# Attention products grouped by tile shape, with scaling tables in PSUM and constants in the opening

## The chip, the cores and the metric

The kernel runs on one core of one Trainium2 chip. The metric is device time in microseconds (us) of one execution, less is better; it is given as the median of several runs.

The engines have these names in the profile: PE is TensorE's matrix products and PEld its weight loads, DVE is VectorE, ACT is ScalarE, POOL is GpSimd, and SP is the engine that issues most of the DMAs here. Each engine works through its own queue in the order in which the program was written.

## The reference

Three layers follow one another: a linear attention with a decaying state, a mixture of 8 experts with one expert per token, and a dense layer. Only the first is touched by the change.

```python
# r, k, v: (4, 8, 768, 48); w, u: (8, 48)
for t in range(S):
    kt, vt, rt = (k[:, :, t], v[:, :, t], r[:, :, t])
    cur = np.einsum('bhd,bhe->bhde', u[None] * kt, vt)
    y[:, :, t] = np.einsum('bhd,bhde->bhe', rt, state + cur)
    state = w[None, :, :, None] * state + np.einsum('bhd,bhe->bhde', kt, vt)
...
# experts: x is y as (3072, 384)
expert_idx = np.argmax(x @ w_gate, axis=1)
out[mask] = gate_w[mask, None] * (np.maximum(xe @ w1[e], 0.0) @ w2[e])
...
# dense: h = x @ w_in;  out = (h - tanh(h)) @ w_out
```

## The kernel before

The attention is computed in chunks of 128 tokens. There are C = 6 chunks and B = 4 batches, and `seq` lists the 24 tiles (chunk, batch) with the batch running fastest. One tile holds all H = 8 heads of 128 tokens, as HP = 4 pairs j of heads with q = 0 or 1 inside a pair. The two heads of a pair lie at partitions 0 to 47 and 64 to 111.

Inside a chunk the products over time become matrix products. For tile n the kernel does this:

- `load` (from SP) brings r, k and v by token into `n_b` (576 KB) and r and k by dimension into `t_b` (two times 192 KB); five buffers each.
- `scale` (VectorE) multiplies r and k by powers of the decay, from the table `PRK` in SBUF, in one instruction over 1024 columns.
- `scores` (TensorE) forms k by r for each head: 64 rows by 128 columns of the array, the two heads of a pair in two PSUM banks `A0` and `A1`. In float32 each product of the program is two matmul instructions in the trace, so 8 products are "x16".
- `side_rk`, `side_rku` and `side_kh` (GpSimd) form r*k, r*k*u and the decayed k, `kh`. `diag_sum` (VectorE) sums r*k*u, and `diag` (ScalarE) puts the sums on the diagonals of `am` with eight instructions. `mask` (VectorE) copies the scores of later tokens over `am`.
- `state` (TensorE) forms kh by v into the PSUM tile `Pp`, which has a bank of its own. VectorE adds it to `sw`, the decayed old state (GpSimd), and keeps the sum in `Sc`. `state_copy` (ScalarE, two instructions) puts it on the blocks of a padded `Sb`.
- `outp` (TensorE) adds two products into `Yp`: inter, from the state of the earlier chunks, `Sb` by `t_b`, as one 128x128 product for each pair; and intra, v by `am`, 128 rows by 48 columns for each head. The two alternate, two pairs at a time. ScalarE copies `Yp` out in two instructions at its end.

For each chunk of four tiles there follow `logits`, `logits2` and `gate` (the expert of each token), `rank_mm` and `rank_sel` (the token's place in its expert) and `idx_mm`. `xout` transposes a tile's output on TensorE into a PSUM tile of the pool `X`, from which ScalarE copies it, scaled by the gate, to `xs`, and SP stores it. The pool `X` has two slots and also serves the logits. Through all this `w_split` makes two parts of expert weights for later, a cast on ScalarE and a subtraction on VectorE.

The order is written out by hand (`manual_schedule`). Loop step n (0 to 24) issues, in this order: the load of n + 3; `diag_sum` and `scale` of n + 1; `logits`; `outp(n - 1)` and its state copy; one `xout`; `diag(n + 1)`; `scores`, `mask` and `state` of n; GpSimd's products of n + 2; then `logits2`, `gate`, `rank_mm`, `rank_sel` and `idx_mm` of chunks that have come so far; then a `w_split`. `at_step(n, first, fn)` calls `fn` for a chunk `first` steps after its last tile. `keep_warm` issues products that nothing reads. `consts` and `gate_cols` are 24 small GpSimd instructions, issued in step 1.

After the loop the last chunk's logits, gate and ranks follow, while a first group of tokens already passes through an expert (`head1`, `head2`); then come the other experts and the dense layer, both long runs of products on TensorE.

Of the kernel before, what the change touches and what calls it, by code (L numbers as in the profile page):

```python
# [30 lines left out]
def rwkv_moe_moe_kernel(ctx: ExitStack, tc: tile.TileContext, rk_t, rkv, pk, u, wp1, wp2, out):  # L31
# [170 lines left out]
    Sc = [ap_.tile([P, HP, D], F32, name=f"Sc{b}") for b in range(B)]  # L202
    Sb = [ap_.tile([P, HP, P], F32, name=f"Sb{b}") for b in range(B)]
# [3 lines left out]
    PRK = ap_.tile([P, 2, HP, P], F32, name="PRK")  # L207
# [5 lines left out]
    yh = [psy.tile([P, BANK], F32, tag=f"y{d}", name=f"yh{d}")[:, 0:HEAD] for d in range(KD)]  # L213
    Yp = [t.rearrange("p (j t) -> p j t", t=P) for t in yh[0:2]]
    Pb = yh[2]
    Pp = Pb[:, 0:HP * D].rearrange("p (j d) -> p j d", d=D)
# [52 lines left out]
    def tables():  # L269
# [9 lines left out]
        table(nc.gpsimd, PRK[:, 0], pq[:, :, 0:8], pw[:, :, 0:16])  # L279
# [3 lines left out]
        table(nc.vector, PRK[:, 1], ipq[:, :, 0:8], ipw[:, :, 1:17])  # L283
# [19 lines left out]
    def zero_states():  # L303
        for b in range(B):
            nc.scalar.mul(out=Sb[b], in_=ident.unsqueeze(1).to_broadcast([P, HP, P]), mul=0.0)
# [24 lines left out]
    def side_kh(n):  # L330
        kh = at3.tile([P, H, D], F32, tag="kh", name="kh")
        nc.gpsimd.tensor_tensor(out=kh, in0=n_b[n % NB][:, 1], in1=KT, op=ALU.mult)
        st["kh", n] = kh
# [29 lines left out]
    def state(n):  # L363
        c, b = seq[n]
        if c == C - 1:
            return
        kh = st.pop(("kh", n))
        for j in range(HP):
            for q in range(2):
                nc.tensor.matmul(Pp[64 * q:64 * q + D, j, :], lhsT=kh[:, 2 * j + q, :],  # L370
                                 rhs=n_b[n % NB][:, 2, 2 * j + q, :], start=True, stop=True)
        if c == 0:
            nc.vector.tensor_copy(out=Sc[b], in_=Pp)
        else:
            sw = at2.tile([P, HP, D], F32, tag="sw", name="sw")
            nc.gpsimd.tensor_tensor(out=sw, in0=Sc[b], in1=bc(pq[:, :, 8:9], [P, HP, D]), op=ALU.mult)
            nc.vector.tensor_tensor(out=Sc[b], in0=sw, in1=Pp, op=ALU.add)
        st["S", b] = n

    def state_copy(n):  # L380
        c, b = seq[n]
        if c == C - 1:
            return
        for q in range(2):
            nc.scalar.copy(out=Sb[b][64 * q:64 * q + 64, :, 64 * q:64 * q + D], in_=Sc[b][64 * q:64 * q + 64, :, :])

    def outp(n):
        c, b = seq[n]
        am = st.pop(("am", n))
        for j0 in range(0, HP, 2):  # L390
            for j in (j0, j0 + 1):
                if c > 0:
                    nc.tensor.matmul(Yp[j % 2][:, j // 2, :], lhsT=Sb[b][:, j, :], rhs=t_b[n % NB][:, 0, j, :],
                                     start=True, stop=False)
            for j in (j0, j0 + 1):
                for q in range(2):
                    p0 = 64 * q
                    nc.tensor.matmul(Yp[j % 2][p0:p0 + D, j // 2, :], lhsT=n_b[n % NB][:, 2, 2 * j + q, :],
                                     rhs=am[:, q, j, :], start=(c == 0), stop=True)
        if b == 0:  # L400
            st["y", c] = yp.tile([P, HP, B, P], F32, tag="y", name="y")
        for i in range(2):
            nc.scalar.copy(out=st["y", c].rearrange("p (j i) b t -> p i j b t", i=2)[:, i, :, b, :], in_=Yp[i])

    sm = ps1.tile([P, 512], F32, tag="sm", name="sm")
# [203 lines left out]
    def by_token():  # L609

        with tc.tile_pool(name="slow", bufs=1) as sp:
# [3 lines left out]
            for b in range(B):  # L615
                nc.vector.memset(Sc[b], 0.0)
# [5 lines left out]
            for c in range(C):  # L622
                st["y", c] = yp.tile([P, HP, B, P], F32, tag="y", name="y")
                for b in range(B):
# [5 lines left out]
                    with tc.For_i(0, P, 1) as t:  # L630
# [8 lines left out]
                        nc.vector.tensor_add(out=cur, in0=cur, in1=Sc[b])  # L639
# [7 lines left out]
                        nc.vector.tensor_tensor(out=Sc[b], in0=Sc[b], in1=bc(wcol.unsqueeze(2), [P, HP, D]), op=ALU.mult)  # L647
                        nc.vector.tensor_add(out=Sc[b], in0=Sc[b], in1=kv)
# [12 lines left out]
    with tc.manual_schedule():  # L661
        w_cols()
        identity()
        for i in range(2):
# [8 lines left out]
        zero_states()  # L673
        keep_warm(20)
        later_keys()
        load(2)
# [20 lines left out]
        for t in Yp + [Pp]:  # L697
            nc.vector.memset(t, 0.0)
# [3 lines left out]
        for n in range(NN + 1):  # L702
            if n + 3 < NN:
                load(n + 3)
            if n % 2 == 1 and n // 4 < PRE:
                w_load(n // 4, n // 2 % 2)
            if n + 1 < NN:
                diag_sum(n + 1)
                scale(n + 1)
            at_step(n, 2, logits)  # L710
            if 1 <= n <= NN:
                outp(n - 1)
                if n > 1:
                    state_copy(n - 1)
            for m in XOUT.get(n, (n - LAG,)):
                if m >= 0:
                    xout(m)
            if 0 < n < NN - 1:
                diag(n + 1)
            if n < NN:  # L720
# [5 lines left out]
                else:  # L726
                    if n == 1:
                        state(0)
                    state(n)
            if n == 1:  # L730
                state_copy(0)
            if n + 2 < NN:
# [4 lines left out]
                side_kh(n + 2)  # L737
            at_step(n, 3, logits2)
            at_step(n, 3, gate)
# [663 lines left out]
```

## Time and profile before

| | us |
|---|---|
| median of 3 runs | 817.4 |
| lowest and highest | 816.46, 819.32 |
| the profiled execution, its own time | 815.03 |
| its span, from first to last instruction | 812.9 |
| busy in the span: PE, DVE, ACT, POOL | 780.9, 648.6, 526.0, 450.7 |

The span is 2.1 us shorter than the execution's own time. All starts below are counted from the span's start. In a row of the timeline the first number is the start, the second the length from the first start to the last end of the merged instructions, then come engine, line, operation, the tiles as out<-in, their shapes and the count; an idle time ahead of the group, with what ended it, stands in square brackets. Two groups of one engine can overlap by their pipelines, so the difference of two starts is the surer measure of what a group costs. The granted clock (PEclk) is given as a share of 2.4 GHz; TensorE's two levels here are 1.2 and 2.4 GHz.

### The profile page before, as it was taken

Reading aid. Unit: us, or ns where it says so; the run is one execution under the profiler, and the core shown is the slowest. Engines: PE = TensorE matmul, PEld = TensorE weight load, DVE = VectorE, ACT = ScalarE, POOL = GpSimd, SP = SyncE. Lnnn points to the kernel's source line nnn. Section 1 sums busy time; section 2 is a strip of 40 time slices with the busy share of each in tenths; the row PEclk is TensorE's granted clock in tenths of the full one; section 3 lists DMA queues with packets and bytes.
Section 4 is the critical chain, followed back from the end, with each engine's and each line's share of the span. In section 5 each row is a group of like instructions: output and inputs, shape, how many; then the busy total and the mean of one; then the engine's idle time right before and its main releaser. Section 6 shows DMA issues by size and latency. Waiting matters only on the chain.

```text
span 812.9 us, 14403 instructions
## 1 busy us (share of the span) xinstructions
PE 780.9 (96%) x5052; PEld 699.3 (86%) x5052; DVE 648.6 (80%) x1127; ACT 526.0 (65%) x1135; POOL 450.7 (55%) x438
## 2 busy tenths in 40 slices
PE   7789999899999999999999999999999999999995
PEld 6567776699899999999989999999999999999895
DVE  7798988449888888995498888888888888888991
ACT  8778887426454545545587776776777677677770
POOL 7987885127676776775445544434345354343532
PEclk9999999999999999999999999999999999999998
DMA  8979864236689889995400000001000000000000
GB/s 220 268 205 260 219 200 135 89 92 188 199 223 267 268 207 276 321 240 160 136 1 0 1 10 30 2 0 40 1 1 30 10 1 20 21 1 10 30 1 39
DMA packets 34979, 89.88 MB, mean 111 GB/s; under 512 B 5690, under 2 KB 13022, under 8 KB 34896
## 3 DMA queue, kind: packets, MB, share of 16 engines
q1 hardware_dynamic: 30704, 78.87, 34.2%
q0 software_dynamic: 4192, 9.99, 4.1%
q8 instruction: 42, 0.69, 0.4%
q14 instruction: 41, 0.34, 0.2%
HBM read 73.10 MB, written 15.74 MB: 109 GB/s over the span
## 4 chain that ended last, share of the span: by engine, by line
PE 49%; DVE 2%; issue 1%; POOL 1%; ACT 0%; POOLq 0%; DVEq 0%; ACTq 0%
PE h L1239 24%; PE o L1287 22%; PE y L1013 2%; PE hps L988 1%; DVE t L1260 0%; DVE h L1257 0%; DVE h L1258 0%; DVE h L1256 0%; DVE t L1255 0%; POOL out_dram L1300 0%; POOL g L1276 0%; ACT g L1275 0%; POOLq L1398 0%; ACT z L1243 0%; ACT t L1245 0%
## 5 line engine op out<-in xcount | busy, mean ns | idle before, releaser
L1276 POOL TENSOR_TENSOR g<-t,g 128x512 fp32r<-128x512 f32 x93 | 120.4, 1295 | 176.3 <-ACT g L1275 122.6
L1239 PE MATMUL h<-xb,ring 128*128 128x512 f32 x864 | 215.9, 395 | 0.7 <-DVE t L1260 0.7
L1287 PE MATMUL o<-ring,g 128*128 128x384 f32 x1116 | 209.3, 336 | 0.0
L1287 PEld LDWEIGHTS o<-ring,g 128*128 128x128 f32 x1116 | 196.1, 188 | 8.1
L1239 PEld LDWEIGHTS h<-xb,ring 128*128 128x128 f32 x864 | 161.3, 188 | 31.9 <-DVE t L1260 1.1
L85 POOL TENSOR_TENSOR ring<-stg,ring 128x384 fp32r<-128x384 f32 x102 | 105.0, 1052 | 57.1 <-ACT ring L84 50.2
L1243 ACT ACTIVATE z<-h 128x512 f32<-128x512 f32 x96 | 57.5, 599 | 98.0 <-PE h L1239 97.9
L1013 PE MATMUL y<-h,ring 128*128 128x256 f32 (+7 forms) x576 | 113.9, 342 | 0.0
L988 PE MATMUL hps<-xt,ring 128*128 128x472 f32 (+6 forms) x504 | 106.1, 354 | 1.8 <-DVE xt L977 0.9
L1013 PEld LDWEIGHTS y<-h,ring 128*128 128x128 f32 x576 | 101.4, 188 | 3.2
L1255 DVE TENSOR_TENSOR t<-t,h 128x512 f32<-128x512 f32 x96 | 65.7, 684 | 41.8 <-ACT t L1245 41.3
L988 PEld LDWEIGHTS hps<-xt,ring 128*128 128x128 f32 x504 | 90.5, 188 | 6.0 <-DVE xt L977 1.6
L84 ACT CAST ring<-stg 128x384 fp32r<-128x384 f32 x152 | 70.8, 512 | 19.1 <-DMA stg<-in_wp_dram 18.6
L1260 DVE COPY_PREDICATED t<-mk,h 128x512 f32<-128x512 uint32 x96 | 72.1, 751 | 9.9
L1257 DVE SCALAR_TENSOR_TENSOR h<-s,h 128x512 f32<-128x512 f32 x96 | 66.9, 696 | 11.4 <-ACT g L1275 1.4
L991 ACT ACTIVATE h<-hps 128x256 fp32r<-128x256 f32 (+7 forms) x64 | 32.0, 501 | 58.2 <-PE hps L988 50.7
L1247 ACT ACTIVATE s<-z,gb 128x512 f32<-128x512 f32 x96 | 69.6, 725 | 0.0
L1258 DVE SCALAR_TENSOR_TENSOR h<-z,h 128x512 f32<-128x512 f32 x96 | 66.8, 696 | 3.3
L1249 ACT ACTIVATE mk<-z,gt 128x512 f32<-128x512 f32 x96 | 69.3, 722 | 0.0
L1256 DVE TENSOR_TENSOR h<-h,z 128x512 f32<-128x512 f32 x96 | 66.4, 692 | 0.0
L1275 ACT CAST g<-t 128x512 fp32r<-128x512 f32 x93 | 57.6, 619 | 7.9 <-DVE t L1260 5.7
L344 ACT ACTIVATE am<-ident,dt 128x128 f32<-128x128 f32 x192 | 58.6, 390 | 4.4 <-DVE dt L337 4.2
(233 smaller groups left out, 1112.9 us busy)
## 6 DMA issues: line engine op xcount, KB each, us to landing
stg<-in_wp_dram SPq DMA_DIRECT2D x64, 384.0 KB
n<-in_rkv_dram SPq DMA_DIRECT2D x24, 576.0 KB
d<-in_wp_dram SPq DMA_DIRECT2D x32, 384.0 KB
t<-in_rk_t_dram SPq DMA_DIRECT2D x48, 192.0 KB
wdec<-dcf SPq DMA_DIRECT2D x32, 192.0 KB
xd<-xs SPq DMA_DIRECT2D x24, 192.0 KB
stg<-wdec SPq DMA_DIRECT2D x12, 384.0 KB
wl<-wdec SPq DMA_DIRECT2D x2, 768.0 KB
```

Source lines behind the costliest of these rows:

```text
L84: nc.scalar.copy(out=dst[:, 0, sl], in_=of)
L85: eng.tensor_tensor(out=dst[:, 1, sl], in0=of, in1=dst[:, 0, sl].bitcast(F32), op=ALU.subtract)
L988: nc.tensor.matmul(ps, lhsT=wf(a, kk), rhs=xt[e][b][:, kk, :], start=(n == 0), stop=(n == 8))
L1013: nc.tensor.matmul(yps[d], lhsT=wf(a)[:, d * P:(d + 1) * P], rhs=h2[:, b, :], start=(f == 0 and n == 0), stop=(f == CH1 - 1 and n == 2))
L1239: nc.tensor.matmul(ps, lhsT=wf(a, kk), rhs=xb[j][:, b, kk, :], start=(n == 0), stop=(n == 8))
L1247: nc.scalar.activation(out=s, in_=z, func=ACTF.Square, scale=G_K ** 0.5, bias=gb)
L1249: nc.scalar.activation(out=mk, in_=z, func=ACTF.Relu, scale=-1.0, bias=gt2)
L1257: nc.vector.scalar_tensor_tensor(out=ps, in0=s, scalar=G_K * G_D, in1=ps, op0=ALU.add, op1=ALU.mult)
L1258: nc.vector.scalar_tensor_tensor(out=ps, in0=z, scalar=G_A, in1=ps, op0=ALU.subtract, op1=ALU.mult)
L1260: nc.vector.copy_predicated(out=t, mask=mk.bitcast(U32), data=ps)
L1276: nc.gpsimd.tensor_tensor(out=g[:, 1, :], in0=ww, in1=g[:, 0, :].bitcast(F32), op=ALU.subtract)
L1287: nc.tensor.matmul(ops[q], lhsT=gg[i][:, b, q * P:(q + 1) * P], rhs=wf(a), start=(f == 0 and n == 0), stop=(f == CH2 - 1 and n == 2))
```

## The change

Five things change, all of them in the attention part.

- `outp` issues all inter products first and then all intra ones. Inter now takes the state directly from `Sc`, one 64x48 product for each head, the two heads of a pair on different rows and columns of the array and in the same PSUM bank. `Yp` is one bank with all four pairs. `Sb`, its zeroing and `state_copy` go; `Sc` gets two buffers for each batch. The copy out of `Yp` becomes one instruction, `y_copy`.
- The decay table moves from SBUF to the two PSUM banks `PR` and `PK`, both made on VectorE, and `scale` becomes two instructions.
- `Pp` comes from the pool `X`, and `kh` is padded with zeros from 48 to 64 columns, in three fixed buffers.
- The order within a step changes: `y_copy(n - 2)`, `diag_sum` and `diag` of n + 1 first; then `scores` and `mask`, `scale(n + 1)`, GpSimd's products, `xout`, `logits2`, `rank_mm`, `idx_mm` (one step later than before), `logits`, `state(n)` and only then `outp(n - 1)`; `gate` and `rank_sel` close the step. `state(0)` moves from step 1 to step 0.
- `consts` and `gate_cols` are issued in the opening, before the first tile's products.

```diff
-    Sc = [ap_.tile([P, HP, D], F32, name=f"Sc{b}") for b in range(B)]
-    Sb = [ap_.tile([P, HP, P], F32, name=f"Sb{b}") for b in range(B)]
+    Sc = [[ap_.tile([P, HP, D], F32, name=f"Sc{b}{i}") for i in range(2)] for b in range(B)]
...
+    kh_b = [ap_.tile([P, H, 64], F32, name=f"kh{i}") for i in range(3)]
...
+    Yp, PR, PK = (t.rearrange("p (j t) -> p j t", t=P) for t in yb)
...
-        table(nc.gpsimd, PRK[:, 0], pq[:, :, 0:8], pw[:, :, 0:16])
+        table(nc.vector, PR, pq[:, :, 0:8], pw[:, :, 0:16])
...
-        nc.vector.tensor_tensor(out=t, in0=t, in1=PRK, op=ALU.mult)
+        for i, pw_ in enumerate((PR, PK)):
+            nc.vector.tensor_tensor(out=t[:, i], in0=t[:, i], in1=pw_, op=ALU.mult)
...
+        Pp = ps1.tile([P, HP, P], F32, tag="X", name="Pp", bufs=2)[:, :, 0:D]
         for j in range(HP):
             for q in range(2):
-                nc.tensor.matmul(Pp[64 * q:64 * q + D, j, :], lhsT=kh[:, 2 * j + q, :],
+                nc.tensor.matmul(Pp[64 * q:64 * q + 64, j, :], lhsT=kh[:, 2 * j + q, :],
                                  rhs=n_b[n % NB][:, 2, 2 * j + q, :], start=True, stop=True)
...
-        for j0 in range(0, HP, 2):
-            for j in (j0, j0 + 1):
-                if c > 0:
-                    nc.tensor.matmul(Yp[j % 2][:, j // 2, :], lhsT=Sb[b][:, j, :], rhs=t_b[n % NB][:, 0, j, :],
-                                     start=True, stop=False)
...
+        if c > 0:
+            for j in range(HP):
                 for q in range(2):
                     p0 = 64 * q
+                    nc.tensor.matmul(Yp[p0:p0 + D, j, :], lhsT=Sc[b][(c - 1) % 2][p0:p0 + 64, j, :],
+                                     rhs=t_b[n % NB][p0:p0 + 64, 0, j, :], start=(j == 0), stop=False)
+        for j in range(HP):
+            for q in range(2):
+                p0 = 64 * q
+                nc.tensor.matmul(Yp[p0:p0 + D, j, :], lhsT=n_b[n % NB][:, 2, 2 * j + q, :],
+                                 rhs=am[:, q, j, :], start=(c == 0 and j == 0), stop=(j == HP - 1))
...
         later_keys()
+        consts()
+        gate_cols()
...
+            if n >= 2:
+                y_copy(n - 2)
             if n + 1 < NN:
                 diag_sum(n + 1)
-                scale(n + 1)
-            at_step(n, 2, logits)
-            if 1 <= n <= NN:
-                outp(n - 1)
-                if n > 1:
-                    state_copy(n - 1)
-            for m in XOUT.get(n, (n - LAG,)):
-                if m >= 0:
-                    xout(m)
-            if 0 < n < NN - 1:
-                diag(n + 1)
+                if n > 0:
+                    diag(n + 1)
             if n < NN:
                 scores(n)
                 mask(n)
...
+            if n + 1 < NN:
+                scale(n + 1)
             if n + 2 < NN:
                 side(n + 2)
...
+            for m in XOUT.get(n, (n - LAG,)):
+                if m >= 0:
+                    xout(m)
             at_step(n, 3, logits2)
-            at_step(n, 3, gate)
...
             at_step(n, 4, rank_mm)
+            if n < NN:
+                at_step(n, 6, idx_mm)
+            at_step(n, 2, logits)
+            if n < NN:
+                state(n)
+            if n > 0:
+                outp(n - 1)
...
+            at_step(n, 3, gate)
             at_step(n, 4, rank_sel)
...
-            if n == 1:
-                consts()
-                gate_cols()
```

## Rows read from the trace of the kernel before

**Rows 1.** Windows: stretch, length, busy time of each engine with instructions, granted clock, DMA.

```profile
64.23:134.70 70.47, 66.88 (x824) 50.36 (x823) 63.20 (x130) 57.40 (x176) 54.30 (x53) 1.00 0.76 213
54.00:57.00 3.00, 2.81 (x16) 1.96 (x18) 2.52 (x9) 1.10 (x4) 1.27 (x4) 0.55 0.78 257
```

**Rows 2.** Timeline: TensorE in step 10, from its scores to the next.

```profile
69.20 1.16 PE L353 MATMUL A<-t 64*128 64x128 f32 x16
...
70.79 1.06 PE L422 MATMUL sm<-sel,lt 128*128 128x8 f32 x8
...
71.71 0.69 PE L393 MATMUL yh<-t,Sb 128*128 128x128 f32 x4
...
74.25 0.66 PE L524 MATMUL Xps<-ident,y 128*128 128x128 f32 x4
...
74.84 1.16 PE L353 MATMUL A<-t 64*128 64x128 f32 x16
```

**Rows 3.** Waits, 30 to 145 us: engine, tile, line, releaser; total, times, longest.

```profile
PEld yh L398 <- DVE am L359: 10.9, 21, 1.8
```

**Rows 4.** Timeline: VectorE's gate (first, last) and rank selection (first, last).

```profile
72.57 0.18 DVE L428 TENSOR_REDUCE m<-sm 128x4 f32<-128x32 f32 x1
...
74.99 0.17 DVE L449 TENSOR_TENSOR cum<-cum,s 128x8 f16<-128x8 f16 x1
...
78.62 0.18 DVE L476 TENSOR_TENSOR pr<-sm,OH 128x32 f32<-128x32 f32 x1
...
79.74 0.92 DVE L501 TENSOR_TENSOR ol<-iotaf,lo 128x512 f16<-128x512 f32 x1
```

**Rows 5.** Timeline: GpSimd's state product beside VectorE's mask and beside its scaling.

```profile
65.43 1.35 DVE L359 COPY_PREDICATED am<-mlt,A 128x512 f32<-128x512 uint32 x2
...
66.25 0.51 POOL L376 TENSOR_TENSOR sw<-Sc,pq 128x192 f32<-128x192 f32 x1
...
69.60 1.56 DVE L312 TENSOR_TENSOR t<-t,PRK 128x1024 f32<-128x1024 f32 x1
...
70.04 1.49 POOL L376 TENSOR_TENSOR sw<-Sc,pq 128x192 f32<-128x192 f32 x1
```

**Rows 6.** Groups by line: count, busy us, mean ns of one, idle before.

```profile
L1255 DVE TENSOR_TENSOR t<-t,h 128x512 f32<-128x512 f32 x96 | 65.7, 684 | 41.8 <-ACT t L1245 41.3
...
L344 ACT ACTIVATE am<-ident,dt 128x128 f32<-128x128 f32 x192 | 58.6, 390 | 4.4 <-DVE dt L337 4.2
...
L84 ACT CAST ring<-stg 128x384 fp32r<-128x384 f32 x152 | 70.8, 512 | 19.1 <-DMA stg<-in_wp_dram 18.6
...
L531 ACT ACTIVATE xs<-Xps,gt 128x384 f32<-128x384 f32 x24 | 13.6, 580 | 1.5 <-PE Xps L524 0.4 <-DVE s L448 0.3 <-ACT y L403 0.2
```

**Rows 7.** Timeline: TensorE's intra products in one block, index products, logits.

```profile
22.06 1.08 PE L398 MATMUL yh<-am,n 128*48 128x128 f32 x16
...
59.93 0.36 PE L510 MATMUL sm<-rh,ol 128*128 128x32 f16 x8
...
60.22 1.06 PE L413 MATMUL lps<-y,wgp 128*32 128x512 f32 x8
```

**Rows 8.** Timeline: the opening, warming products, GpSimd's products and constants, VectorE's wait.

```profile
12.88 2.84 PE L543 MATMUL warm<-ident 128*128 128x128 f32 x24
...
15.97 1.01 POOL L317 TENSOR_TENSOR rk<-n 128x384 f32<-128x384 f32 x1 [1.55 <-DMA n<-in_rkv_dram]
...
18.02 3.90 POOL L332 TENSOR_TENSOR kh<-n,KT 128x384 f32<-128x384 f32 x3
...
24.85 0.22 POOL L145 MEMSET ones<- 128x128 f16 x1
...
27.90 0.99 POOL L317 TENSOR_TENSOR rk<-n 128x384 f32<-128x384 f32 x1
...
30.00 0.55 DVE L337 TENSOR_REDUCE dt<-rku 128x8 f32<-128x384 f32 x1 [2.52 <-POOL rku L323]
```

**Rows 9.** Timeline: the last output products of the attention part.

```profile
148.39 0.64 PE L398 MATMUL yh<-am,n 128*48 128x128 f32 x8
```

More of the change, by code (lines that the diff above doesn't have):

```diff
@@ L206, in rwkv_moe_moe_kernel @@
     pq = ap_.tile([P, HP, 9], F32, name="pq")
-    PRK = ap_.tile([P, 2, HP, P], F32, name="PRK")
     ipw = ap_.tile([P, HP, 17], F32, name="ipw")
@@ L212, in rwkv_moe_moe_kernel @@
     KT = ap_.tile([P, H, D], F32, name="KT")
[L213 to L216, printed above, removed]
+    kh_b = [ap_.tile([P, H, 64], F32, name=f"kh{i}") for i in range(3)]
+    yb = [psy.tile([P, BANK], F32, tag=f"y{d}", name=f"yh{d}") for d in range(KD)]
+    yh = [t[:, 0:HEAD] for t in yb]
+    Yp, PR, PK = (t.rearrange("p (j t) -> p j t", t=P) for t in yb)
     headn = ap_.tile([P, 1], F32, name="headn")
@@ L282, in tables @@
         nc.vector.tensor_tensor(out=ipl, in0=ipq, in1=bc(pq[:, :, 8:9], [P, HP, 9]), op=ALU.mult)
-        table(nc.vector, PRK[:, 1], ipq[:, :, 0:8], ipw[:, :, 1:17])
+        table(nc.vector, PK, ipq[:, :, 0:8], ipw[:, :, 1:17])
     def table(eng, dst, fa, fb):
@@ L301, in zero_pad @@
             eng.memset(dst, 0.0)
-    def zero_states():
-        for b in range(B):
-            nc.scalar.mul(out=Sb[b], in_=ident.unsqueeze(1).to_broadcast([P, HP, P]), mul=0.0)
     st = {}
@@ L330, in side_kh @@
     def side_kh(n):
-        kh = at3.tile([P, H, D], F32, tag="kh", name="kh")
-        nc.gpsimd.tensor_tensor(out=kh, in0=n_b[n % NB][:, 1], in1=KT, op=ALU.mult)
+        kh = kh_b[n % 3]
+        nc.gpsimd.tensor_tensor(out=kh[:, :, 0:D], in0=n_b[n % NB][:, 1], in1=KT, op=ALU.mult)
         st["kh", n] = kh
@@ L367, in state @@
         kh = st.pop(("kh", n))
+        Pp = ps1.tile([P, HP, P], F32, tag="X", name="Pp", bufs=2)[:, :, 0:D]
         for j in range(HP):
             for q in range(2):
-                nc.tensor.matmul(Pp[64 * q:64 * q + D, j, :], lhsT=kh[:, 2 * j + q, :],
+                nc.tensor.matmul(Pp[64 * q:64 * q + 64, j, :], lhsT=kh[:, 2 * j + q, :],
                                  rhs=n_b[n % NB][:, 2, 2 * j + q, :], start=True, stop=True)
+        new = Sc[b][c % 2]
         if c == 0:
-            nc.vector.tensor_copy(out=Sc[b], in_=Pp)
+            nc.vector.tensor_copy(out=new, in_=Pp)
         else:
             sw = at2.tile([P, HP, D], F32, tag="sw", name="sw")
[L376 to L385, printed above, removed]
+            nc.gpsimd.tensor_tensor(out=sw, in0=Sc[b][(c - 1) % 2], in1=bc(pq[:, :, 8:9], [P, HP, D]), op=ALU.mult)
+            nc.vector.tensor_tensor(out=new, in0=sw, in1=Pp, op=ALU.add)
     def outp(n):
@@ L663, in rwkv_moe_moe_kernel @@
         identity()
+        for t in kh_b:
+            nc.gpsimd.memset(t[:, :, D:], 0.0)
         for i in range(2):
@@ L696, in rwkv_moe_moe_kernel @@
         side(1)
-        for t in Yp + [Pp]:
-            nc.vector.memset(t, 0.0)
+        nc.vector.memset(Yp, 0.0)
         nc.gpsimd.memset(cum[0], 0.0)
```

29 lines of the change are left out of this document (10 added, 19 removed).

## The prediction

> **What bounds the kernel now.** I read the page first, then the windows, the waits and the timeline of the attention part, which is all that the change touches. It takes the first 149.03 us (the last output product starts at 148.39 and lasts 0.64 us [rows 9]); what follows hangs on its last output, so I count a shift of that end one to one. From the scores of step 9 to those of step 21 TensorE is busy 66.88 us of 70.47, VectorE 63.20, ScalarE 57.40, GpSimd 54.30 [rows 1]: 23.5 us for four steps, and two engines near full. The reader is to see that no single engine is the bound; the chain passes from one to another. In one step of TensorE the scores and the state take 1.59 us, logits2 0.92, the output 2.54, the transposes 0.59 [rows 2]. With the index products (0.36) and the logits (1.06) [rows 7], and the rank products put at the nearest row, the same 0.36, four steps are 4 x 4.72 + 2.70 = 21.6 us of work. The other 1.9 are mostly the output waiting for its masked scores: weight loads waited 10.9 us on that in 21 places [rows 3], because the mask is made late in VectorE's queue and the output of the same step comes right behind the scores.
>
> **The change, part by part.**
>
> **Output products.** The inter product becomes 16 matmuls of 64x48 instead of 8 of 128x128, in one block, and so do the 16 intra ones. A block of 16 intra was 1.08 us [rows 7]. The 16 inter ones are in no trace. From below, 16 small products cost 0.5 (scores and state together are 1.59, the scores alone 1.16 to their last result [rows 2]); from above, twice the scores, 2.2, if the two tiles of a pair did not run together. The nearest row is the scores themselves, 16 products of 64 rows over 128 columns, about 1.1. I take 1.0, the new weights having 48 columns, so output = 2.05, 0.5 less than 2.54. The state's weights grow from 48 to 64 columns: between 0 and a third of its 0.5; I take 1.65 for scores and state.
>
> Here a rule of the Trainium skill speaks against the change. The trace shows pairs running together where two row tiles write different banks (the scores, A0 and A1) or two column tiles write one bank (intra, state); two row tiles writing one bank it does not show. TensorEngine Tiling (Array Packing), section Restrictions and Gotchas, says that different row tiles cannot access the same PSUM bank simultaneously. By that rule inter would not pair and the sum would be that of the second rival, 831, against 814.6 with pairs.
>
> **The wait on the mask goes.** The output of step n-1 now stands at the end of step n, so its mask is a step old. What is late next is VectorE and, every fourth step, ScalarE (below).
>
> **VectorE and GpSimd.** The decay table moves to two PSUM banks, scaling becomes two instructions. Before, one scaling took 1.56 us while a GpSimd product beside it took 1.49 instead of 0.51 [rows 5]; beside the mask, which reads PSUM, GpSimd took its 0.51. A product with a PSUM operand over 512 columns takes 0.684 [rows 6], so two are 1.37, and I expect no blocking. VectorE's five operations of every step stand back to back between gate and rank selection: the gate ends at 75.16, the selection starts at 78.62 [rows 4], so 3.46; I take 3.5, of which mask and scale 2.6 and add, split, sum 0.9. The gate is 2.59, the selection 78.62 to 80.66, 2.04 [rows 4]. The state copies leave ScalarE, which is not the bound there.
>
> **The state's PSUM bank** now comes from the two-slot pool of transposes and logits. In the step with logits three tiles pass through two slots, so the state waits until ScalarE has emptied the transposes; and that copy now stands behind the next step's diagonals: 58.6/24 = 2.44 us, then the copy 0.58 [rows 6]. This is a new wait, and TensorE's output, queued behind the state, pays it.
>
> **The recurrence.** Call S(n) the start of the scores of step n. Scores, mask, scale, next scores is a loop of 1.2 + 2.6 = 3.8 us. The four kinds of step:
> A (indices, logits; n = 9, 13, 17): VectorE adds, splits behind ScalarE's cast and sums by +1.9; diagonals and copy make it 4.9; state 0.55, output 2.05: 7.5 us, against 5.7 of TensorE's own work.
> B (logits2, gate): 1.65 + 0.59 + 0.92 + 2.05 = 5.2.
> B and C: VectorE's loop, gate and round: 3.8 + 2.6 + 3.5 = 9.9, so C = 4.7 (TensorE 4.65).
> D: 3.5 + 2.04 + a cast of 0.51 [rows 6] that now waits behind GpSimd's share of the selection = 6.05.
> Sum 23.45, against 23.5. The gain on the mask is given back to the slots.
>
> **The opening.** The state of step 0 now precedes the 12 warming products. Its operand kh is GpSimd's first after the products of tile 2, whose data come at 15.97; the three kh start at 18.02 and take 3.90 [rows 8], one about 1.0, so 19.0. State 0.5, then warming: 2.84 us [rows 8] at 2.4 GHz, twice that at 1.2; TensorE has idled some 6 us by then, so I take the middle, 4.2. S(1) = 23.7, between 22.4 and 25.2. From there steps are 3.8, not held by GpSimd: the constants, 24.85 to 27.90, were on its path (VectorE waited 2.52 us for its product at 30.00 [rows 8]) and now lie where GpSimd waited for data. If that cover failed they would cost up to 3.05. S(5) = 23.7 + 15.2 = 38.9; step 5 (no transposes) 1.65 + 1.06 + 2.05 = 4.75, so S(6) = 43.65; S(8) = S(6) + 9.9 = 53.55; S(9) = 59.6, against 64.23 [rows 1]: 4.6 us earlier. Loads now wait for the output at a step's end; they have from S(n) to the product of step n+1, a step or more, which I cost at nothing; at the 3.8 us steps that is the thinnest cover, and a load late by 1 us would cost about 1 us.
>
> **The rest.** Three rounds from 59.6 at 23.45, less 1.2 for the splits that end at step 18: S(21) = 128.75 (134.70 [rows 1]). Step 21 has two transposes, so the logits wait: 0.5 + 2.44 + 0.58 + 1.06 + 2.05 = 6.6. Step 22: 1.1 + 0.92 + 2.05 = 4.1. The last: scores 1.1, transposes 1.2, ranks 0.36, two outputs 4.1: 6.75. End 146.2, against 149.03: 2.8 us less. The profiled execution took 815.03 us, 2.4 below the median of 817.4; taken from either it is the same step: 812.2 there, 814.6 on the median. A measurement of this kernel can tell about 0.3%, 2.5 us, from no change. The forecast's own range adds 1.4 for S(1), 0.25 for each of 12 outputs that TensorE sets, and the load's 1 us: 809.5 to 819.
>
> **Rivals.**
> 1. The slot wait is hidden: ScalarE's diagonals come early enough. For it: GpSimd and VectorE block each other less, so sums come earlier. Against: the order of ScalarE's queue. A is then 5.7: 3 x 1.8 and 2 in step 21, 7.4 more: 807.
> 2. Inter tiles of one bank run one after another: inter is 2.05, output 3.1. It decides once TensorE sets the step: A and B pay 1.05 each, C 1.05, D (5.35 under 6.05) nothing: 3 x 3.15, 3.1 in steps 5 to 8 and 4.2 after step 20, 16.6: 831, slower. For it: no row of two row tiles on one bank. Against: the pair writes different partitions, as the column tiles do. By the skill's rule above, this is the case.
> 3. The clock falls in A. The slot wait leaves TensorE idle about 1.8 us (3.1 to 4.9 of the step). After the longest wait on a mask, 1.8 us [rows 3], the stretch 54 to 57 was granted 0.55 [rows 1], mostly the lower of the two levels. State and output, 2.6 us, at such a clock take 2.6 x (1/0.55 - 1) = 2.1 more, in each of four steps (9, 13, 17, 21) 8.5 us: 823, slower. It decides once such a wait makes the clock fall. Against: most waits of a microsecond left the clock at 1.00.
>
> **How the numbers follow.** Chances: the forecast 0.48, rival 1 0.20, rival 2 0.12, rival 3 0.20. The forecast stands on the border, so it gives faster 0.25, same 0.20, slower 0.03; rival 1 faster 0.20; rival 2 slower 0.12; rival 3 slower 0.15, same 0.05: faster 0.45, same 0.25, slower 0.30. The range runs from just under rival 1 to just above rival 3, 806 to 826; it leaves out rival 2 and little of the others.
>
> **What would show it.** Right: no wait of output products on the mask; scaling near 1.37 with no GpSimd product stretched beside it; S(9) near 59.6; four steps about 23.5, with the state of steps 9, 13, 17 waiting for the transposes' copy; 16 inter products in about 1.0. Wrong: four steps at 22 or less (rival 1), 16 inter products at 2 (rival 2), granted clock near 0.5 in steps 9, 13, 17 (rival 3), or GpSimd waiting for loads, which none of this counts.

## The result, and the profile after

The changed kernel takes 824.4 us (median of 4 runs, 823.1 to 825.6) against 816.9 for the kernel before on the same chip: a ratio of 1.0089, interval 1.0068 to 1.0109. It is 7.4 us slower, where the forecast was 2.8 us faster; 824.4 lies inside the stated range of 806 to 826, but on the other side of the kernel before. Its profiled execution took 823.76 us, with a span of 821.8 (before: 815.03 and 812.9).

The attention part now ends at 156.05 us instead of 149.03. That is 7.0 of the 8.9 us by which the span grew; the other 1.9 lie behind it. (For every kernel but the one before, this document takes as the end the start of the next product, 0.07 us ahead of the last output product's own end.) The quickest reading is a list of the starts of each step's scores, S(n), set beside the prediction's own sums.

| stretch, us | before | predicted | after | after less predicted |
|---|---|---|---|---|
| start to S(1) | 18.40 | 23.7 | 26.27 | +2.57 |
| S(1) to S(8) | 39.94 | 29.85 | 30.21 | +0.36 |
| step 8 | 5.89 | 6.05 | 7.53 | +1.48 |
| S(9) to S(21) | 70.47 | 69.15 | 73.92 | +4.77 |
| S(21) to the end of attention | 14.33 | 17.45 | 18.12 | +0.67 |
| end of attention | 149.03 | 146.2 | 156.05 | +9.85 |

So the early steps gained what was forecast (9.7 us from S(1) to S(8)), the opening and the end lost more than was forecast (7.9 and 3.8), and the three rounds in the middle, forecast 1.3 shorter, became 3.45 longer.

First the busy time of the engines on the page of the kernel after: share of the span, instructions.

```profile
PE 771.0 (94%) x5212; PEld 698.9 (85%) x5212; DVE 640.4 (78%) x1150; ACT 508.5 (62%) x1067; POOL 431.3 (52%) x440
```

Every engine did less work than before (TensorE 780.9, VectorE 648.6, ScalarE 526.0, GpSimd 450.7). The change did what it says; the loss is waiting. Windows of the kernel after show the three rounds (against [rows 1]), the opening and the middle of step 9:

```profile
64.01:137.93 73.92, 60.77 (x916) 49.90 (x916) 58.59 (x143) 48.84 (x142) 46.72 (x53) 0.98 0.73 214
...
12.00:21.00 9.00, 1.47 (x10) 1.07 (x12) 3.54 (x9) 5.25 (x17) 5.86 (x8) 0.50 1.03 232
69.00:72.00 3.00, 2.99 (x38) 2.54 (x40) 1.28 (x3) 0.83 (x2) 2.79 (x3) 0.61 0.87 232
```

In the three rounds TensorE is busy 60.77 us instead of 66.88, VectorE 58.59 instead of 63.20, ScalarE 48.84 instead of 57.40 and GpSimd 46.72 instead of 54.30, and yet the stretch is 3.45 us longer. TensorE idles 13 us in it where it had idled 3.6. Who it waits for stands in the waits of the kernel after, 0 to 155 us (engine, tile, line, releaser; total, times, longest):

```profile
ACT am L342 <- DVE dt L335: 26.9, 18, 4.2
POOL rk L315 <- DMA n<-in_rkv_dram: 21.5, 14, 3.9
PEld Pp L369 <- ACT xs L528: 9.0, 3, 3.1
PE Pp L369 <- ACT xs L528: 6.2, 3, 2.2
```

No wait on the mask is among them any more [rows 3]. In its place stand the state's wait for ScalarE's copy of the transposes in the three steps that also have logits (9, 13 and 17), and GpSimd waiting 21.5 us in 14 places for the loads by token; before, that was 4.2 us in 2 places. ScalarE's diagonals wait 26.9 us for VectorE's sums, which need GpSimd's products; before, that was 4.2 [rows 6]. The timeline of the kernel after, TensorE and ScalarE in steps 9 and 10, shows the first of these and what the products now cost (against [rows 2]):

```profile
64.01 1.25 PE L351 MATMUL A<-t 64*128 64x128 f32 x16 [1.70 <-issue]
...
65.97 1.07 PE L410 MATMUL lps<-y,wgp 128*32 128x512 f32 x8
66.04 2.45 ACT L342 ACTIVATE am<-ident,dt 128x128 f32<-128x128 f32 x8 [0.67 <-DVE dt L335]
68.40 0.56 ACT L528 ACTIVATE xs<-Xps,gt 128x384 f32<-128x384 f32 x1
69.01 0.67 PE L369 MATMUL Pp<-n,kh 128*64 128x48 f32 x16 [1.97 <-ACT xs L528]
69.61 1.91 PE L387 MATMUL yh<-t,Sc 64*48 64x128 f32 x16
71.45 1.86 PE L392 MATMUL yh<-am,n 128*48 128x128 f32 x16
73.24 1.16 PE L351 MATMUL A<-t 64*128 64x128 f32 x16
...
75.72 0.67 PE L369 MATMUL Pp<-n,kh 128*64 128x48 f32 x16
76.32 1.08 PE L387 MATMUL yh<-t,Sc 64*48 64x128 f32 x16
77.32 1.08 PE L392 MATMUL yh<-am,n 128*48 128x128 f32 x16
78.33 1.16 PE L351 MATMUL A<-t 64*128 64x128 f32 x16
```

In step 10 the 16 inter products take 1.00 us (76.32 to 77.32) and the 16 intra ones 1.01: the output is 2.0 us, as forecast. In step 9 the state waits 1.97 us for `xs`, which stands in ScalarE's queue behind eight diagonals of 2.45 us, which themselves waited for VectorE's sum. Behind that idle time the granted clock is 0.61 in the window 69 to 72, mostly the lower level, and the output takes 3.6 us instead of 2.0. In steps 13 and 17 the same wait (2.04 in step 13) left the clock at 1.00.

The next timeline of the kernel after is step 8, with the rank selection: GpSimd, VectorE and TensorE.

```profile
52.95 0.55 DVE L85 TENSOR_TENSOR ring<-stg,ring 128x384 fp32r<-128x384 f32 x1
...
53.52 1.00 POOL L315 TENSOR_TENSOR rk<-n 128x384 f32<-128x384 f32 x1 [2.94 <-DMA n<-in_rkv_dram]
...
56.48 1.25 PE L351 MATMUL A<-t 64*128 64x128 f32 x16 [0.29 <-PE yh L392]
...
56.53 0.51 POOL L376 TENSOR_TENSOR sw<-Sc,pq 128x192 f32<-128x192 f32 x1
57.07 0.35 DVE L377 TENSOR_TENSOR Sc<-sw,Pp 128x192 f32<-128x192 f32 x1 [0.70 <-POOL sw L376]
...
59.72 1.31 DVE L85 TENSOR_TENSOR ring<-stg,ring 128x384 fp32r<-128x384 f32 x1 [0.32 <-DMA xd<-xs]
...
62.63 1.27 DVE L310 TENSOR_TENSOR t<-t,yh 128x512 f32<-128x512 f32 x2
...
64.01 1.25 PE L351 MATMUL A<-t 64*128 64x128 f32 x16 [1.70 <-issue]
```

GpSimd waits 2.94 us for a load; its next three products and then `sw`, the decayed old state, come later by that; VectorE's add waits for `sw`, and everything that VectorE has to do for the next tile waits behind the add. The scores of step 9 start 0.11 us after the end of VectorE's scaling of that tile (62.63, 1.27 us long): the 1.70 us of idle time before them, for which the profile names no releaser ("issue"), are TensorE waiting for VectorE. In this kernel VectorE waited for `sw` itself in two places only, 1.4 us in all.

### The profile page after: what moved, and what is told of

Read it like the earlier page. It is cut to its first block, busy times and chain, and to the rows that moved or that the text cites. A ratio compares the mean times of both kernels' runs of the same rounds, so it can differ in the third digit from the quotient of the medians.

```text
span 821.8 us, 14670 instructions
## 1 busy us (share of the span) xinstructions
PE 771.0 (94%) x5212; PEld 698.9 (85%) x5212; DVE 640.4 (78%) x1150; ACT 508.5 (62%) x1067; POOL 431.3 (52%) x440
## 4 chain that ended last, share of the span: by engine, by line
PE 48%; DVE 2%; issue 1%; POOL 1%; ACT 0%; POOLq 0%; DVEq 0%; ACTq 0%
PE h L1236 23%; PE o L1284 22%; PE y L1010 2%; PE hps L985 1%; DVE t L1257 0%; DVE h L1254 0%; DVE h L1255 0%; DVE h L1253 0%; DVE t L1252 0%; POOL out_dram L1297 0%; POOL g L1273 0%; ACT g L1272 0%; POOLq L1395 0%; ACT z L1240 0%; ACT t L1242 0%
## 5 line engine op out<-in xcount | busy, mean ns | idle before, releaser
L342 ACT ACTIVATE am<-ident,dt 128x128 f32<-128x128 f32 x192 | 58.8, 389 | 27.0 <-DVE dt L335 26.9
```

## The experiments

The theory after the result had three parts. (a) The slot wait in the steps with indices and logits, as in the prediction, is not offset by anything. (b) The late loads hold GpSimd, and its `sw`, queued behind the products of a later tile, passes that on to VectorE. (c) The state of tile 0 ahead of the warming products costs more in the opening than was forecast. The rivals: the new inter products or the padded state are slow in themselves; the scaling tables in PSUM gain nothing; the constants in the opening cost something.

| kernel | built on | median us | ratio to before, interval | S(1) | S(8) | end of attention |
|---|---|---|---|---|---|---|
| before | | 816.9 | | 18.40 | 58.34 | 149.03 |
| after | | 824.4 | 1.0068 to 1.0109 | 26.27 | 56.48 | 156.05 |
| e1_own_bank | after | 822.0 | 1.0050 to 1.0101 | 26.75 | 57.23 | 156.07 |
| e2_act_order | after | 817.4 | 0.9997 to 1.0032 | 26.85 | 57.07 | 150.25 |
| e3_state0_late | after | 826.1 | 1.0084 to 1.0144 | 17.70 | 57.35 | 157.82 |
| e4_consts_alone | before | 813.5 | 0.9944 to 0.9975 | 18.57 | 56.58 | 148.43 |
| e5_act_state0 | e2 | 813.3 | 0.9943 to 0.9992 | 18.47 | 54.34 | 144.33 |
| e6_state0_alone | after | 822.6 | 1.0052 to 1.0108 | 17.97 | 53.09 | 153.05 |
| e7_decay_first | e5 | 809.4 | 0.9894 to 0.9950 | 18.25 | 51.41 | 140.84 |
| e8_no_token_loads | after | 821.3 | 1.0043 to 1.0098 | 25.20 | 54.86 | 150.39 |
| e9_table_sbuf | e7 | 813.0 | 0.9923 to 0.9962 | 17.48 | 54.37 | 145.40 |
| e10_consts_late | e7 | 808.5 | 0.9870 to 0.9934 | 18.01 | 51.64 | 141.20 |
| e11_decay_alone | after | 823.2 | 1.0056 to 1.0120 | 23.85 | 53.51 | 152.62 |
| e12_state_bank | after | 823.8 | 1.0059 to 1.0114 | 25.60 | 59.37 | 155.66 |

The median of the kernel before was 816.2 to 816.9 in all these comparisons, so medians of different rows can be set side by side. But the runs of one kernel spread by 2.5 to 10 us, so two medians that differ by less than about 2.5 us (an estimate) are not told apart. The last three columns are of the one profiled execution.

**The slot wait: the state in another bank.**

```diff
-        Pp = ps1.tile([P, HP, P], F32, tag="X", name="Pp", bufs=2)[:, :, 0:D]
+        Pp = sm[:, 320:320 + HP * D].rearrange("p (j d) -> p j d", d=D)
```

> The changed kernel, but the state's product goes to 192 free columns of the bank sm instead of the two-slot pool X, so that it no longer waits for ScalarE's copy of the transposes. Theory 'slots' (the loss sits in steps 9, 13 and 17, where TensorE waited 2.0 to 2.2 us for that copy): these steps fall from 9.2, 7.7 and 7.9 us to about 5.8, the granted clock stays at 1.00 there, and the time falls by 6 to 8 us to about 817. Theory 'loads' (GpSimd's waits for loads hold VectorE, and TensorE's slot wait only lies beside that): under 2 us less. Theory 'opening' (the loss is the 8 us later start of step 1): under 2 us less.

Measured: 822.0 us, 2.4 less than after, at the edge of what can be told apart. Steps 9, 13 and 17 take 8.73, 7.08 and 7.83, no shorter to speak of (9.23, 7.68, 7.85). The timeline of e1_own_bank says why, VectorE and TensorE in step 9:

```profile
69.15 0.18 DVE L510 COPY idf<-sm 128x32 f32<-128x32 f32 x1
69.38 0.67 PE L369 MATMUL sm<-n,kh 128*64 128x48 f32 x16 [1.78 <-DVE idf L510]
```

The bank `sm` also holds the result of the index products. The state, which writes other columns of it, now waited for VectorE's copy of them, for 1.78 us in place of 1.97. One wait took the place of the other; this run didn't separate the theories.

**The slot wait: ScalarE's order.** The diagonals of the next tile go behind the copy of the transposes.

```diff
                 diag_sum(n + 1)
-                if n > 0:
-                    diag(n + 1)
...
                     xout(m)
+            if 0 < n < NN - 1:
+                diag(n + 1)
```

> The changed kernel, but ScalarE's eight diagonals of the next tile are issued behind the copy of the transposes instead of ahead of it. Theory 'slots': the slot comes free about 2.4 us earlier, steps 9, 13 and 17 fall to about 6, step 21 from 6.8 to about 5.6, and the time falls by 6 to 8 us, as with a bank of its own. Theory 'loads' and theory 'opening': under 2 us less.

Measured: 817.4 us, 7.0 less than after. Timeline of e2_act_order, TensorE and ScalarE in step 9:

```profile
66.34 0.58 ACT L528 ACTIVATE xs<-Xps,gt 128x384 f32<-128x384 f32 x1 [1.02 <-issue]
66.82 2.43 ACT L342 ACTIVATE am<-ident,dt 128x128 f32<-128x128 f32 x8
67.37 0.67 PE L369 MATMUL Pp<-n,kh 128*64 128x48 f32 x16
67.97 1.08 PE L387 MATMUL yh<-t,Sc 64*48 64x128 f32 x16
68.98 1.08 PE L392 MATMUL yh<-am,n 128*48 128x128 f32 x16
```

The state no longer waits, and step 9 takes 5.57 us; 13 and 17 take 7.05 and 5.58, and 21 takes 5.57 (6.78 after). The 5.7 of the prediction's first rival is the step without the wait. In step 13 the logits took 1.94 us instead of 1.06, behind an idle time of 1.69 ahead of the scores; the granted clock from 88 to 91 us was 0.53.

**The opening: state(0) later.** The state of tile 0 goes back to step 1, in the place where the other states are issued.

```diff
-            if n < NN:
+            if n == 1:
+                state(0)
+            if 0 < n < NN:
                 state(n)
```

> The changed kernel, but the state of tile 0 is issued in step 1, behind the scores of tile 1, as before the change; the 12 warming products then follow the transposes of the table without waiting for GpSimd. Theory 'opening': step 1 starts at 18 to 20 instead of 26.3, the granted clock stays at 1.00 until 20 us, and 3 to 5 us of it are left at step 8, so the time falls by 3 to 5. Theory 'slots': step 1 starts earlier, but loads and VectorE take it back before step 9, under 2 us less.

Measured: 826.1 us. S(1) came back to 17.70, as expected, but S(2) was 28.31. `kh` has three fixed buffers; in that place the products of tile 3 are already issued ahead of state(0), so the state of tile 0 is formed from tile 3's operand, and waits for it. The run says that S(1) hangs on state(0), and nothing on what the opening costs in all.

**Only the constants, in the kernel before.**

```diff
         later_keys()
+        consts()
+        gate_cols()
...
-            if n == 1:
-                consts()
-                gate_cols()
```

> The kernel before with one part of the change alone: the constants and gate columns are made in the opening. If GpSimd is what holds steps 3 and 4 of the kernel before (VectorE waited 2.52 us for its product in step 3), those steps start 2 to 3 us earlier and the time falls by 2 to 3 us against before. If loads or VectorE take that back within the following steps, no difference beyond 1 us.

Measured: 813.5 us, 2.7 less than before (0.25 to 0.56%). S(3) and S(4) were within 0.5 us of those before (29.65 and 34.07 against 29.17 and 34.32); the attention part of its profiled execution ended 0.5 us earlier, and that execution took 815.07, the longest of its ten. Where the 2.7 us of the median lie is therefore not shown. That the constants cost nothing in the opening is shown: the data of tile 2 came at 16.47 and S(1) is 18.57.

**Both: ScalarE's order and the opening.** To e2_act_order, state(0) in step 1 again, now ahead of GpSimd's products of tile 3.

```diff
                     diag(1)
+            if n == 1:
+                state(0)
             if n + 1 < NN:
                 scale(n + 1)
...
-            if n < NN:
+            if 0 < n < NN:
                 state(n)
```

> The changed kernel with two of its orders mended: the diagonals behind the copy of the transposes (as in e2_act_order) and the state of tile 0 in step 1, between the scores and the scaling of that step, so that its operand is still tile 0's. Theory 'slots and opening' (both cost): step 1 starts near 18 instead of 26.9, step 8 near 51 to 53 instead of 57, and the time falls 4 to 6 us under e2_act_order, to about 812, below the kernel before. Theory 'loads': the transfers, which already filled the DMA engines up to 50 us in the kernel before, hold steps 5 to 9, and less than 2 us of the earlier start is left.

> The changed kernel with only the state of tile 0 moved back into step 1 (between the scores and the scaling of that step). Theory 'opening': 4 to 6 us less than the changed kernel, about 819. Theory 'loads': under 2 us less.

Measured: e5 813.3 us, 4.1 less than e2_act_order; e6, which is state(0) without ScalarE's order, 822.6, 1.8 less than after. S(1) is 18.47 (26.85 in e2) and 17.97 (26.27 in after), so 8 us at the start become 3.4 (e6) and 2.7 (e5) at S(8), and 1.8 and 4.1 in the medians (the 1.8, with runs from 818.3 to 825.5, is not told apart from nothing): the steps that follow are held by something else. In e6 steps 9, 13 and 17 are 7.91, 7.50 and 8.85; in e5 they are 5.58, 5.57, 5.58. The timeline of e5_act_state0 shows what holds the early steps, GpSimd and VectorE in step 5:

```profile
34.93 1.01 POOL L315 TENSOR_TENSOR rk<-n 128x384 f32<-128x384 f32 x1 [0.75 <-DMA n<-in_rkv_dram]
...
37.93 0.52 POOL L376 TENSOR_TENSOR sw<-Sc,pq 128x192 f32<-128x192 f32 x1
...
38.48 0.35 DVE L377 TENSOR_TENSOR Sc<-sw,Pp 128x192 f32<-128x192 f32 x1 [2.27 <-POOL sw L376]
```

VectorE stood still for 2.27 us because `sw` stood behind three products of tile 7 that waited for their load; the step took 6.40.

**The decay ahead of the products.** To e5, `sw` issued on GpSimd before the products of tile n + 2; its operand is a chunk old, so nothing holds it there.

```diff
+    def decay(n):
+        c, b = seq[n]
+        if 0 < c < C - 1:
+            sw = at2.tile([P, HP, D], F32, tag="sw", name="sw")
+            nc.gpsimd.tensor_tensor(out=sw, in0=Sc[b][(c - 1) % 2], in1=bc(pq[:, :, 8:9], [P, HP, D]), op=ALU.mult)
+            st["sw", n] = sw
...
                 scale(n + 1)
+            if n < NN:
+                decay(n)
             if n + 2 < NN:
```

> As e5_act_state0, and GpSimd decays the old state ahead of the products of tile n + 2 instead of behind them, so that VectorE's addition no longer stands behind a product that waits for a load. Theory 'loads through the addition': VectorE's waits for that product (2.6 us in four places with the diagonals moved) go and the steps with rank selection fall by 0.5 to 0.7 us each, 1 to 3 us less than e5_act_state0. If VectorE's own queue sets these steps, no difference beyond 1 us.

> The changed kernel with one order mended alone: GpSimd decays the old state ahead of the products of tile n + 2. Theory 'loads through the addition': steps 8, 12 and 16 (7.5, 6.5, 6.9 us) fall by 0.5 to 1 us each and the steps with the gate before them by less, 2 to 4 us less than the changed kernel, 820 to 822. If the slot wait takes this back in steps 9, 13 and 17, under 1 us.

Measured: e7 809.4 us, 3.8 less than e5, 7.4 less than before and 14.9 less than after: this version beats both kernels. Timeline of e7_decay_first, VectorE's add in step 7, and the window of its three rounds:

```profile
51.24 0.34 DVE L383 TENSOR_TENSOR Sc<-sw,Pp 128x192 f32<-128x192 f32 x1
```

```profile
58.15:123.85 65.70, 59.26 (x915) 48.83 (x916) 59.25 (x143) 48.34 (x141) 46.57 (x54) 1.00 0.84 244
```

The add waits for nothing any more, and step 5 takes 4.79 us. The gain in the attention part lies mostly in S(1) to S(8): 33.16 us against 35.87 in e5; S(8) to S(21) is 72.44 against 73.09. The three rounds take 65.70, where the kernel before took 70.47 and after 73.92. Alone on top of after (e11), the same edit gave 823.2, 1.2 less and not told apart from nothing: steps 9, 13 and 17 are still 8.41, 7.92 and 7.84. Its attention part ended 3.4 us earlier, of which 2.4 is already in S(1) (below), but its span is only 0.4 shorter: the part behind the attention took the rest back, and the cause of that stays open.

**The loads by token left out.**

```diff
-        nc.sync.dma_start(out=rkv_t, in_=rkv[b, c])
+        if n < NB:
+            nc.sync.dma_start(out=rkv_t, in_=rkv[b, c])
```

> The changed kernel without the loads by token (r, k and v, 576 KB a tile) of tiles 5 to 23: those tiles use what the buffers hold from tiles 0 to 4, so the output is another. This takes away GpSimd's waits for them (12.3 us in eight places between 40 and 140 us). Theory 'loads': 4 us less or more than that. Theory 'slots': steps 9, 13 and 17 stay at 7.5 to 9, and the time falls by under 2 us.

Measured: 821.3 us, 3.1 less than after. GpSimd's wait for loads falls from 21.5 to 1.9 us, both in the opening, while steps 9, 13 and 17 keep 7.91, 7.85 and 7.84. The loads, with the traffic that they bring, are worth 3.1 us with the slot wait and the early state(0) in place, and the slot wait doesn't come from them. The attention part of the profiled execution ended 5.7 us earlier. Of this, 1.1 lie ahead of S(1), where these loads play no part, and 1.3 in step 9, where the lower clock fell on the scores and logits instead of the output; 1.9 are in the steps with the rank selection (6.71, 6.26, 6.51 and 5.14 instead of 7.53, 6.48, 6.86 and 5.65).

**The table back in SBUF.** In e7, `PRK` in SBUF and one scaling over 1024 columns, as before the change.

```diff
-        for i, pw_ in enumerate((PR, PK)):
-            nc.vector.tensor_tensor(out=t[:, i], in0=t[:, i], in1=pw_, op=ALU.mult)
+        nc.vector.tensor_tensor(out=t, in0=t, in1=PRK, op=ALU.mult)
```

> As e7_decay_first, but the decay table lies in SBUF again and the scaling is one instruction. Theory 'table': with the table in PSUM the scaling was 1.27 us with nothing beside it stretched; in SBUF it is about 1.5 us and stops GpSimd's product beside it for about a microsecond. VectorE sets half of the steps, so 12 to 16 of them lengthen by 0.3 to 0.5 us: 4 to 7 us more than e7_decay_first's 809.4. If GpSimd's stop also holds the decayed state, more. If the table's place matters little, under 2 us.

Measured: 813.0 us, 3.6 more than e7. Groups by line, 0 to 150 us (count, busy us, mean ns of one, idle before), of e7_decay_first and then of e9_table_sbuf:

```profile
L310 DVE TENSOR_TENSOR t<-t,yh 128x512 f32<-128x512 f32 x48 | 30.4, 673 | 0.0
L330 POOL TENSOR_TENSOR kh<-n,KT 128x384 f32<-128x384 f32 x24 | 25.7, 1072 | 0.0
```

```profile
L310 DVE TENSOR_TENSOR t<-t,PRK 128x1024 f32<-128x1024 f32 x24 | 35.8, 1493 | 0.2 <-DMA t<-in_rk_t_dram 0.2
L330 POOL TENSOR_TENSOR kh<-n,KT 128x384 f32<-128x384 f32 x24 | 41.3, 1724 | 0.0
```

With the table in SBUF one scaling takes 1.49 us instead of 2 x 0.673, and the GpSimd product that runs beside it takes 1.72 us instead of 1.07. So the tables in PSUM, with the scaling in two instructions, are worth 3.6 us here: they pay on both engines, as [rows 5] had suggested. The Trainium skill (SBUF — State Buffer, section Who interferes with whom) says that a VectorE instruction with two SBUF inputs contends with a GpSimd instruction that reads SBUF, and one with at most one SBUF input, outside its two-port modes, doesn't; these two groups agree with both halves.

**The constants back in step 1.** In e7, `consts` and `gate_cols` where they were before.

> As e7_decay_first, but the constants and gate columns are made in step 1 again. Theory 'constants': GpSimd is on the path in steps 1 to 4 there as well, so 2 to 3 us more than 809.4. If loads hold these steps anyway, under 1 us.

Measured: 808.5 us, 1 less than e7 and not told apart from it. In that order of work the place of the constants makes no difference that these runs can tell.

**The state in a bank of its own.** To after, the table in SBUF, as in e9, which leaves a bank free for `Pp` alone.

```diff
-        Pp = ps1.tile([P, HP, P], F32, tag="X", name="Pp", bufs=2)[:, :, 0:D]
+        Pp = PK[:, :, 0:D]
```

> The changed kernel with the decay table back in SBUF (one scaling instruction) and the state's product alone in one of the two banks that this frees, so that it waits for neither the transposes' copy nor any other reader; ScalarE's order is as in the changed kernel. Theory 'slots' (it is the slot that couples the state to ScalarE): TensorE's waits for the copy (6.2 us in three places) go, steps 9, 13 and 17 fall to 5.7 to 6.5 us; with the slots worth 7 us (as e2_act_order had it) and the table costing 3.6 (as e9_table_sbuf had it) the time is 820 to 822. Theory 'ScalarE's order by itself' (its late diagonals hold those steps whatever bank the state has): these steps stay at 7.5 or more, and the time is 826 to 829.

Measured: 823.8 us, 0.6 less than after and above what was expected. Timeline of e12_state_bank, TensorE in step 9:

```profile
69.09 0.67 PE L369 MATMUL yh<-n,kh 128*64 128x48 f32 x16
69.69 1.08 PE L387 MATMUL yh<-t,Sc 64*48 64x128 f32 x16
70.70 1.08 PE L392 MATMUL yh<-am,n 128*48 128x128 f32 x16
71.71 0.38 PE L351 MATMUL A<-t 64*128 64x128 f32 x2
```

The wait is gone, and steps 9, 13 and 17 take 5.57, 5.65 and 5.58, with the diagonals where the change had put them: what held them was the shared slot together with ScalarE's order, and either cure removes it. What the table in SBUF took elsewhere shows in the waits of e12_state_bank, 40 to 140 us:

```profile
DVE Sc L377 <- POOL sw L376: 9.2, 14, 2.3
```

`sw` took 1.24 us on average (0.51 after), and VectorE waited 9.2 us for it. That e9 lost only 3.6 by the same table fits its `sw` being issued early; that this is the whole difference is argued, not shown.

## Why the prediction was wrong, by its own steps

The attention part ended 9.85 us later than the sum said. To a tenth each: 2.6 in the opening, 0.4 from S(1) to S(8), 3.5 in the steps with the rank selection, 0.8 in the steps with rank products behind them, 2.3 in the steps with the slot wait, 0.7 at the end, less 0.3 in the steps with the gate. The loads, put at nothing, stand behind a part of several of these.

**Right.** The output products: 16 inter in 1.00 us and 16 intra in 1.01, so 2.0 where 2.05 was taken. The second rival had priced inter at 2.05, one product after another; two row tiles that write different partitions of one bank run together here. The Trainium skill (TensorEngine Tiling (Array Packing), section Restrictions and Gotchas) says that they can't; this measurement decides, and the second rival falls. Scores and state are 1.16 to 1.25 and 0.6 us: the 64 columns cost 0.1 at most. Scaling was forecast at 0.684 each and is 0.674. The wait on the mask is gone. S(1) to S(8) was forecast at 29.85 and took 30.21, with the loop of scores, mask, scale in most steps near its 3.8. The steps with logits2 and the gate took 5.09 (5.2).

**The slot wait: right in kind and cause and nearly in size, the clock came on top.** The prediction put steps 9, 13 and 17 at 7.5, and they took 9.23, 7.68 and 7.85, 2.3 us more in sum. The state started 5.00, 5.06 and 5.23 us after the scores, where 4.9 was forecast: 0.6 of the 2.3. Another 1.6 is the output of step 9 at the lower clock. Here rival 3 was right in its mechanism and wrong in its count: it had four such steps, and one had it. That its time, 823, is near the measured 824.4 is therefore no proof of it, and that 824.4 lies in a range drawn up to 826 for this rival is luck. e2_act_order and e12_state_bank show the wait's cause from two sides.

**Steps with the rank selection: the term that was mis-sized by most.** 6.05 was forecast; steps 8, 12, 16 and 20 took 7.53, 6.48, 6.86 and 5.65 (the last without a split, forecast 4.85), 3.5 us more in sum. The sum took add, split and sum as 0.9 us back to back. The row of step 8 shows the split alone at 1.31 us, beside GpSimd's product, behind a wait of 0.32, and the add waiting 0.70 for `sw`. The same split took 0.55 us at 52.95, while GpSimd stood waiting; its two operands lie in SBUF, as those of the scaling in [rows 5] did, so the change took this blocking from the scaling and left it on the split. Without the loads by token these steps are still 0.2 to 0.7 us over the forecast (e8). The steps that followed, with rank products, had 0.8 more in sum for the three (4.63, 4.62 and 5.64 against 4.7).

**The loads: the step that failed outright.** The prediction costed them at nothing, while saying that at steps of 3.8 us the cover was thinnest and naming GpSimd's waits for them among its signs of being wrong. GpSimd waited for them 21.5 us instead of 4.2, and since `sw` is issued behind the products that wait, VectorE pays. The prediction named the queue for ScalarE (diagonals ahead of the copy) but never asked what stands behind GpSimd's waiting product. What VectorE paid directly is small in the changed kernel, 1.4 us, and larger once the other two waits are mended: 4.6 us in four places in e5. Without these loads the kernel is 3.1 us faster (e8); with `sw` ahead of them e5 becomes 3.8 us faster (e7). On after alone the same edit gave nothing that can be measured (e11), with the slot wait still in its place.

**The opening: right in kind, 2.6 us too small.** S(1) was 26.27. The data of tile 2 arrived late, and TensorE had idled, as the timeline of the kernel after shows (against [rows 8]):

```profile
17.57 1.00 POOL L315 TENSOR_TENSOR rk<-n 128x384 f32<-128x384 f32 x1 [2.12 <-DMA n<-in_rkv_dram]
20.65 1.10 PE L369 MATMUL Pp<-n,kh 128*64 128x48 f32 x16 [7.00 <-POOL kh L330]
21.67 4.67 PE L540 MATMUL warm<-ident 128*128 128x128 f32 x24
```

The data came at 17.57 and not 15.97 (1.6); the state took 1.0 and not 0.5; the warming products took 4.67 and not 4.2. The first varies from execution to execution: in e11_decay_alone, whose program is the same up to there, they came at 15.83 and S(1) was 23.85, the 23.7 of the forecast. That is the lowest of five executions with this opening (after, e1, e2, e8, e11: 23.85 to 26.85), so the forecast sat at their lower edge. The larger error is of another kind: the 5.3 us that the prediction itself gave away here were a choice of the change, needed by nothing else in it. With state(0) in step 1 and ScalarE's order, 4.1 us come back (e5).

**The end.** Step 21 with its slot wait was 6.78 (6.6), step 22 4.10 (4.1), the last 7.24 (6.75). Before, S(21) to the end took 14.33: of the 3.8 us more, 1.2 are step 21's slot wait (5.57 without it in e2); the other 2.6 are put down to an output that comes a step late, which no run took back. The forecast had 3.1 of the 3.8.

**One to one behind the attention: not quite.** The span less the end of the attention part is 663.9 before and 665.8 after, 664.4 in e7 and 665.4 in e2. The forecast took it as fixed; 1.9 us of the longer span lie there. But this is one execution of each kernel: over the fourteen profiled ones it is 663.7 (e1) to 669.1 (e3), and the profiled execution of the kernel before was 1.9 us under its median, so it is not shown that the medians differ by it. In 156 to 230 us the granted clock is 0.95 after and 0.98 before, and GpSimd's gather of tokens waits 14.7 us in one place for VectorE's list of them. What sets that was not tried.

**The parts don't add.** Against after, ScalarE's order alone gives 7.0, state(0) in step 1 alone 1.8, `sw` first alone 1.2, all three 14.9. The sum of the parts is 10.0, with an uncertainty of some us; the ends of the attention part point the same way, 5.8, 3.0 and 3.4 us earlier against 15.2 for all three. The reading is that each is in part hidden behind another as long as that stands: steps 9, 13 and 17 keep 7.5 us or more in e6 and e11. The forecast's own sum, in which each step's longest term was taken by itself, had no such coupling in it but the one of ScalarE. (Its own range, by the terms that it names, would be 810.2 to 820.0 and not 809.5 to 819; nothing hangs on that.)

## What to carry to other kernels

When a change reorders a step, list for each in-order queue what stands behind every instruction that can wait, and ask who waits for that: here a small product (`sw`, 0.51 us) behind three that depend on a load, and a copy (0.58 us) behind eight diagonals, together with a state issued too early in the opening, cost 14.9 us, where the change without these three orders gains 7.4 (e7). A tile that borrows a slot or some columns of a shared PSUM bank inherited the readers of its neighbours as waits in these kernels (1.78 us in e1, 1.97 to 2.2 us in after), so a borrowed bank is checked against every engine that reads from it. An engine's busy time that falls on all four engines is no evidence of a shorter span; test such a change in parts, and in combination too, since one wait can hide the gain of removing another.

## What was unexpected of the hardware

Products of 64x48 on two row tiles and two column groups, writing different partitions of one bank, ran in pairs: 1.00 us for 16 in step 10.

The same idle time ahead of TensorE's products didn't always have the same effect on the clock: in the kernel after 1.97 us ahead of the state in step 9 was followed by a granted clock of 0.61, 2.04 us in step 13 by 1.00. Ahead of them TensorE had idled 1.31 and 1.70 us in step 8, and 0.34 and 1.70 in step 12; but 1.04, 1.37 and then 2.21 us ahead of the state in step 17 left the clock at 1.00 too, so what decides is not shown. In the opening, with TensorE nearly idle (1.47 of 9 us busy), the clock was 0.50, and 24 warming products then took 4.67 us where they had taken 2.84.
